# One order of slots from the first unit on, in a fused top-k attention and cosine feed-forward kernel

## The chip, the cores and the metric

The kernel runs on one core of one Trainium2 chip. Five engines work side by side, each through its own queue in order: TensorE (PE in the profile; PEld is its weight load), VectorE (DVE), ScalarE (ACT), GpSimd (POOL) and SyncE (SP), which here only issues DMA transfers. They wait for each other through semaphores. The metric is the time of one execution on the device in microseconds (us). Four executions of the kernel before took 1467.71, 1468.69, 1468.35 and 1466.98, median 1468.03. The profiled one is that of 1467.71, with a span of 1465.9 from its first to its last instruction.

## The reference, cut to what matters

```python
# q, k, v: (8 batches, 8 heads, 576 rows, 64), float32
scores = scale * np.matmul(q, k.transpose(0, 1, 3, 2))
kth = np.partition(scores, -top_k, axis=-1)[..., -top_k:-top_k + 1]      # top_k = 32
scores = np.where(scores >= kth, scores, -1000000000.0)
attn = np.exp(scores - np.max(scores, axis=-1, keepdims=True))
attn = attn / (np.sum(attn, axis=-1, keepdims=True) + 1e-09)
attn_out = np.matmul(attn, v).astype(np.float32)
# to (4608 tokens, 512), then
h = x @ w_in            # w_in (512, 2048)
g = h * np.cos(h)
out = g @ w_out         # w_out (2048, 512)
```

The two weight matrices reach the kernel as 64-bit floating point numbers, read as pairs of 32-bit words.

## The kernel before

**Units.** The tokens are cut into 36 tiles of 128, and the 8 heads into 4 pairs (NP = 4). A unit is one tile and one pair of heads, 144 in all (NU). A unit's scores are 128 x 2 x 576 numbers. Feed-forward work goes by blocks of 128 tokens, four units each: 8 first pieces (ff1, line 518: 16 matmul records to the profile's count) and 8 second pieces (ff2, line 599).

**Slots.** The order of the work is written out by hand: the loop at the end runs slots 0 to 144, and in slot i unit u = i is searched on VectorE, while unit w = i - 1 goes through its mask, exponentials and sums. Each engine runs its part of a slot in the order of the text. Three functions write slots: early_slot (line 696) for slots 0 to EARLY = 2 * NP = 8, slot (line 740) to LAST = 140, last_slot (line 787) for the rest.

**The search.** VectorE folds the 576 scores of a row into 288 maxima (fold_high, line 244) and 288 minima ("low"). It searches the maxima in four rounds of MAX8 and MATCH_REPLACE8 (lines 349 and 354, rounds 0 to 3 of topk_round), then the minima in two, and merges (lines 337 and 342). The minima are made in one of two ways: by VectorE from the scores in PSUM (fold_now, line 252), for units 0 to EARLY; or by GpSimd as sum minus maximum (fold_sum, line 262, and fold_low, line 271), for later units. ScalarE copies scores out of PSUM (take_scores, lines 233 and 234), masks (line 380) and exponentiates (line 388).

**Transposing the attention weights.** The product with v needs them transposed. For units before EARLY and the last four, transposes_now does it in the next slot: GpSimd normalises (line 409), TensorE transposes nine times (line 448), ScalarE copies to pT (lines 452, 455) and the product back out (line 485). For the others ("paired"), the way is through memory, two slots later: GpSimd splits the words in halves (split, lines 421 and 423), SP writes them to device memory (rows, line 431) and reads them back with a transposing DMA into pT (line 437, three buffers). Their values are then made by twos in every even slot (z: units i - 4 and i - 3), and VectorE multiplies them out by the reciprocal sums (take_values, line 483).

**Decoding the weights.** There are 32 chunks of 128 x 512 numbers: 16 of w_in, 16 of w_out. Each is loaded into one of 7 staging buffers (load_weights, line 102). Then decode_first: ScalarE turns the high words (line 128). decode_second: GpSimd rounds the low words (line 138) and VectorE shifts the high ones left by three (line 141). decode_third: GpSimd adds the two (line 151). early_slot handles three chunks a slot, two from slot 6 on; slot handles two.

**Feed-forward.** feed (line 643) issues pieces as a credit, their operands and the chunks decoded allow. After a first piece ScalarE takes the bank (lines 548 and 550), GpSimd reduces (570, 579), ScalarE takes the sine (589, with a table load to and fro) and GpSimd multiplies (gate, line 596); a second piece may follow.

In slot, the weights' steps stand here:

```python
        take_scores(units[i + 1])
        if w and not late:
            exponentials(w)
        decode_second(2)
        topk_round(u, 3, both(w), z)
        ...
        gate(1)
        ...
        decode_third()
        decode_first(2)
        reduce_first()
```

Of the kernel before, what the change touches and what calls it, by code (L numbers as in the profile page):

```python
# [30 lines left out]
def kernel(  # L31
# [62 lines left out]
    CHUNKS, XB = 7, 4  # L94
    ff = {"live": 0, "tick": 0, "now": 0, "credit": 0.0, "end": False, "kind": 0, "half": 0, "open": 0}
# [26 lines left out]
    def decode_first(n):  # L122


        for _ in range(min(n, len(wq["loaded"]))):
            st, w = wq["loaded"].popleft()
            hi = st[:, :, 1]
            nc.scalar.activation(
                out=w, in_=hi.bitcast(F32), func=AF.Prelu, scale=2.0**-111, alpha=2.0**32
            )  # L130
            wq["second"].append((st, w))

    def decode_second(n):

        for _ in range(min(n, len(wq["second"]))):
            st, w = wq["second"].popleft()
            wi, lo = w.bitcast(I32), st[:, :, 0]
            nc.gpsimd.tensor_scalar(
                out=lo, in0=lo.bitcast(U32), scalar1=2.0**-29, scalar2=1.0, op0=ALU.mult, op1=ALU.mult
            )  # L140
# [97 lines left out]
    def fold_high(u):  # L238

        s, sc = u["s"], u["sc"]  # L240
        if u["n"] > EARLY:
            del u["sc"]
# [23 lines left out]
    def fold_low(u):  # L266

        if not u["folds"]:
            return
# [19 lines left out]
    def topk_first(u, w):  # L289
# [5 lines left out]
        if u["folds"]:  # L295
            if u["n"] > EARLY:
                fold_sum(u)
# [5 lines left out]
        if u["folds"] and u["n"] <= EARLY:  # L303
            fold_now(u)
# [364 lines left out]
    EARLY, LAST = 2 * NP, NU - NP  # L669
    scored, last, last_values = {}, {}, {}  # L670
    for i, u in enumerate(units):
        two = i % 2 == 0 and EARLY + 2 < i < LAST + 2 and (len(u["parts"]) == 1 or u["hp"] == 0)
# [6 lines left out]
    for n in range(NP, len(order)):  # L679
        i = last[order[n - 5]] if n >= 5 else 0  # L680
        at_slot.setdefault(max(i, NP + 2), []).append((load_qk, *order[n]))
        i = last_values[order[n - 6]] if n >= 6 else 0
        at_slot.setdefault(max(i + 4 - i % 2, NP + 2), []).append((load_v, *order[n]))
# [7 lines left out]
    for i, u in enumerate(units):  # L691
        u["n"] = i
        u["folds"] = i < LAST + 2
        u["paired"] = EARLY <= i < LAST

    def early_slot(i, u, w):
        n = 3 if i < 6 else 2
        topk_first(u, w)
        if i == 0:
            decode_second(1)  # L700
        scores(units[i + 1])
        for load, b, hp in at_slot.get(i, []):
            load(b, hp)
        load_weights(n)
        if w:
            mask(w)
            exponentials(w)
        topk_round(u, 1)

        decode_second(n)  # L710
        topk_round(u, 2, both(w))
        topk_round(u, 3)
        if w:
            normalise(w)
        take_banks()
        take_scores(units[i + 1])
        gate(1)
        decode_third()
        feed(2)
        reduce_first()  # L720
        reduce_second()
        if i != NP:
            decode_first(n - 1)
        if w:
            transposes_now(w)
        feed(1)
# [170 lines left out]
```

## Time and profile before

| what | value |
|---|---|
| time, median of 4 | 1468.03 us (1466.98 to 1468.69) |
| the profiled execution's own time | 1467.71 us |
| its span | 1465.9 us |
| busy TensorE, VectorE, ScalarE, GpSimd | 1402.0, 1367.2, 1078.0, 1159.5 us |
| slots 0, 4, 8, 12, 16 start (first fold, line 244) at | 7.04, 52.72, 98.39, 142.96, 185.9 us |
| mean granted TensorE clock | 0.973 |

How to read it: a line of the timeline has the start, the length, the engine, the line of the kernel, the operation and its tiles, xN for N of them in a row, and in brackets how long the engine stood idle before it and what ended that. A line of a group has the total, the mean of one in ns, and the idle time before it with its releasers. A line by stretches has the busy time of each engine in that stretch. A busy TensorE is not TensorE at its peak, since matmuls overlap.

### The profile page before, as it was taken

Reading aid. Unit: us, or ns where it says so; the run is one execution under the profiler, and the core shown is the slowest. Engines: PE = TensorE matmul, PEld = TensorE weight load, DVE = VectorE, ACT = ScalarE, POOL = GpSimd, SP = SyncE. Lnnn points to the kernel's source line nnn. Section 1 sums busy time; section 2 is a strip of 40 time slices with the busy share of each in tenths; the row PEclk is TensorE's granted clock in tenths of the full one; section 3 lists DMA queues with packets and bytes.
Section 4 is the critical chain, followed back from the end, with each engine's and each line's share of the span. In section 5 each row is a group of like instructions: output and inputs, shape, how many; then the busy total and the mean of one; then the engine's idle time right before and its main releaser. Section 6 shows DMA issues by size and latency. Waiting matters only on the chain.

```text
span 1465.9 us, 30361 instructions
## 1 busy us (share of the span) xinstructions
PE 1402.0 (96%) x10360; PEld 1012.4 (69%) x10360; DVE 1367.2 (93%) x5209; ACT 1078.0 (74%) x1908; POOL 1159.5 (79%) x836
## 2 busy tenths in 40 slices
PE   4678899999999999999999999999999999999998
PEld 3565577777777767777777767777777777777765
DVE  7999999999999999999999999999999999999831
ACT  4666677777777777777777777777777787777651
POOL 4669888888888887888888888888888888888410
PEclk6688899999999999999999999999999999999999
DMA  8524576666664577557765667666666566655200
GB/s 278 153 90 141 149 200 162 156 162 187 174 174 143 150 196 181 159 145 189 190 166 142 159 171 197 168 147 168 194 176 152 149 161 176 168 152 147 66 8 15
DMA packets 405547, 229.53 MB, mean 157 GB/s; under 512 B 355088, under 2 KB 371728, under 8 KB 405392
## 3 DMA queue, kind: packets, MB, share of 16 engines
q1 hardware_dynamic: 399984, 217.93, 55.6%
q10 hardware_dynamic: 5408, 9.65, 1.8%
q8 instruction: 82, 1.34, 0.4%
q14 instruction: 73, 0.60, 0.1%
HBM read 45.09 MB, written 95.94 MB: 96 GB/s over the span
## 4 chain that ended last, share of the span: by engine, by line
PE 84%; DVE 6%; ACT 5%; DMA 2%; POOL 1%; issue 1%; SPq 1%; ACTq 0%; POOLq 0%
PE mm L534 32%; PE o L609 31%; PE rim L474 11%; PE sc L223 7%; DVE top L349 3%; PE rim L223 2%; DVE rest L354 2%; ACT s L388 1%; DMA v<-in_v_dram 1%; ACT s L380 1%; PE tp L448 1%; ACT L388 1%; ACT s L233 0%; DVE w_out L141 0%; DMA st<-in_moe_w_in_dram 0%
## 5 line engine op out<-in xcount | busy, mean ns | idle before, releaser
L534 PEld LDWEIGHTS mm<-xT,w_in 128*128 128x128 f32 x4608 | 540.4, 193 | 71.9 <-issue 65.8
L609 PE MATMUL o<-w_out,g 128*128 128x512 f32 x1152 | 541.1, 603 | 9.0 <-POOL g L596 6.0
L534 PE MATMUL mm<-xT,w_in 128*128 128x128 f32 x4608 | 543.0, 276 | 3.4 <-DVE xT L483 1.9
L349 DVE MAX8 top<-rest 128x8 f32<-128x288 f32 x1148 | 481.3, 454 | 0.0
L421 POOL COPY halves<-s 128x2304 uint16<-128x2304 uint16 x132 | 277.6, 2103 | 150.2 <-ACT s L388 150.0
L354 DVE MATCH_REPLACE8 rest<-top,rest 128x288 f32<-128x288 f32 (+1 forms) x860 | 376.9, 445 | 0.0
L609 PEld LDWEIGHTS o<-w_out,g 128*128 128x128 f32 x1152 | 203.4, 191 | 198.4 <-issue 186.6
L349 DVE MAX8 top<-low 128x8 f32<-128x288 f32 x568 | 239.3, 448 | 2.7 <-POOL low L271 2.7
L388 ACT ACTIVATE s<-s,nd 128x576 f32<-128x576 f32 x288 | 220.1, 766 | 0.8
L380 ACT ACTIVATE s<-s,top 128x576 f32<-128x576 f32 x288 | 206.1, 766 | 0.0
L271 POOL TENSOR_TENSOR low<-low,rest 128x576 int32<-128x576 int32 x133 | 187.8, 1412 | 10.4
L262 POOL TENSOR_TENSOR low<-s 128x576 int32<-128x576 int32 x133 | 187.6, 1411 | 1.3 <-DVE rden L401 1.3
L548 ACT ACTIVATE g<-mm 128x512 f32<-128x512 f32 x144 | 85.8, 596 | 130.5 <-PE mm L534 124.5
L474 PE MATMUL rim<-pT,v 128*64 128x128 f32 (+1 forms) x2560 | 161.9, 271 | 9.0 <-ACT pT L455 9.0
L579 POOL TENSOR_TENSOR x<-g,x 128x1024 f32<-128x1024 f32 x68 | 160.8, 2365 | 5.7
L596 POOL TENSOR_TENSOR g<-g,x 128x1024 f32<-128x1024 f32 x68 | 160.8, 2365 | 2.3 <-ACT x L589 2.3
L223 PE MATMUL sc<-k,q 64*128 64x448 f32 (+1 forms) x640 | 151.5, 584 | 9.2 <-DMA k<-in_k_dram 9.2
L474 PEld LDWEIGHTS rim<-pT,v 128*64 128x64 f32 x2560 | 134.3, 140 | 20.5 <-ACT pT L455 11.4
L233 ACT COPY s<-sc 128x896 f32<-128x896 f32 x144 | 129.2, 897 | 3.5 <-PE sc L223 3.0
L354 DVE MATCH_REPLACE8 low<-top,low 128x288 f32<-128x288 f32 x284 | 123.5, 443 | 0.0
L234 ACT COPY s<-rim 128x256 f32<-128x256 f32 x144 | 55.0, 382 | 84.9 <-PE rim L474 84.9
L244 DVE TENSOR_TENSOR rest<-sc,s 128x576 f32<-128x576 f32 x142 | 106.2, 748 | 6.1 <-ACT s L234 6.0
(59 smaller groups left out, 1323.0 us busy)
## 6 DMA issues: line engine op xcount, KB each, us to landing
rows<-halves SPq DMA_DIRECT2D x132, 640.0 KB, 3.0
out_dram<-ob ACTq DMA_DIRECT2D x36, 256.0 KB, 2.1
q<-in_q_dram SPq DMA_DIRECT2D x31, 288.0 KB, 3.9
st<-in_moe_w_in_dram SPq DMA_DIRECT2D x16, 512.0 KB, 6.0
v<-in_v_dram SPq DMA_DIRECT2D x32, 256.0 KB, 3.3
st<-in_moe_w_out_dram SPq DMA_DIRECT2D x16, 512.0 KB, 3.8
k<-in_k_dram SPq DMA_DIRECT2D x31, 144.0 KB, 3.6
k<-in_k_dram SPq DMA_DIRECT2D x32, 128.0 KB, 3.7
```

Source lines behind the costliest of these rows:

```text
L223: nc.tensor.matmul(to[r0 : r0 + rows, j, 0 : k1 - k0], st["q"][d, q0 : q0 + rows], st["k"][d, k0:k1], start=True, stop=True,)
L262: nc.gpsimd.tensor_tensor(out=u["low"].bitcast(I32), in0=s[:, :, 0:HS], in1=s[:, :, HS:S], op=ALU.add)
L271: nc.gpsimd.tensor_tensor(out=low, in0=low, in1=u["rest"][:, :, HS:S].bitcast(I32), op=ALU.subtract)
L349: nc.vector.max(to[:, j], src[:, j])
L354: nc.vector.match_replace(rest[:, j], to[:, j], src[:, j], NEG)
L380: nc.scalar.activation(out=s[:, j], in_=s[:, j], func=AF.Prelu, bias=less[:, j, 1:2], scale=1.0, alpha=FAR)
L388: nc.scalar.activation(out=s[:, j], in_=s[:, j], func=AF.Exp, bias=nd[:, j : j + 1], scale=SCALE, accum_out=den[:, j, 0:1],)
L421: nc.gpsimd.tensor_copy(out=halves[:, :, 0 : 2 * S], in_=s.rearrange("p (k h) -> p h k", h=2))
L474: nc.tensor.matmul(o[d, to], lhsT, rhs, start=c == 0, stop=c == NT)
L534: nc.tensor.matmul(mm[:, at : at + w], w_in[f // FC][:, c, (f % FC) * P : (f % FC + 1) * P], blk["xT"][:, c], start=c == 0, stop=c == NC - 1,)
L579: nc.gpsimd.tensor_tensor(out=x, in0=g, in1=x, op=ALU.subtract)
L609: nc.tensor.matmul(o, g[:, at : at + P], w_out[f], start=f == 0, stop=f == NF - 1)
```

## The change

- early_slot is gone; slot writes all slots up to 140. So units 0 to 7 too are transposed through memory, their values made by twos, two to three slots later, and multiplied out by VectorE; scores are made by twos from unit 4 on.
- The minima of units 7 to 10 (BUSY) are made by VectorE; those of all other units up to 141, the first seven included, by GpSimd.
- The low words of a chunk are rounded by ScalarE, in decode_first, in place of GpSimd in decode_second.
- All slots handle up to three chunks. Shifts and adds (decode_second, decode_third) now follow each other directly, behind round 2, that is behind the third of the four rounds; the adds stand ahead of the gate and reductions.
- In the first four slots the loads of q, k and v stand ahead of the chunks. Loads of the second batch are due from slot 10, not 6. Sines move to their later place from slot 12 on, not 16.

```diff
+    BUSY = range(7, 11)
...
-            hi = st[:, :, 1]
+            lo, hi = st[:, :, 0], st[:, :, 1]
             nc.scalar.activation(
                 out=w, in_=hi.bitcast(F32), func=AF.Prelu, scale=2.0**-111, alpha=2.0**32
             )
+            nc.scalar.mul(out=lo, in_=lo.bitcast(U32), mul=2.0**-29)
...
-            wi, lo = w.bitcast(I32), st[:, :, 0]
-            nc.gpsimd.tensor_scalar(
-                out=lo, in0=lo.bitcast(U32), scalar1=2.0**-29, scalar2=1.0, op0=ALU.mult, op1=ALU.mult
-            )
+            wi = w.bitcast(I32)
...
-        if u["n"] > EARLY:
+        if u["n"] not in BUSY:
             del u["sc"]
...
-        if not u["folds"]:
+        if not u["folds"] or u["n"] in BUSY:
             return
...
-            if u["n"] > EARLY:
+            if u["n"] not in BUSY:
                 fold_sum(u)
...
-        if u["folds"] and u["n"] <= EARLY:
+        if u["folds"] and u["n"] in BUSY:
             fold_now(u)
...
-        two = i % 2 == 0 and EARLY + 2 < i < LAST + 2 and (len(u["parts"]) == 1 or u["hp"] == 0)
+        two = i % 2 == 0 and 2 < i < LAST + 2 and (len(u["parts"]) == 1 or u["hp"] == 0)
...
-        at_slot.setdefault(max(i, NP + 2), []).append((load_qk, *order[n]))
+        at_slot.setdefault(max(i, 2 * NP + 2), []).append((load_qk, *order[n]))
...
-        u["paired"] = EARLY <= i < LAST
-
-    def early_slot(i, u, w):
...
+        u["paired"] = i < LAST
...
     def slot(i, u, w, x, z):
-        load_weights(2)
+        n = 3
+        if i < NP:
+            for load, b, hp in at_slot.pop(i, []):
+                load(b, hp)
+        load_weights(n)
         if x:
             send(x)
         topk_first(u, w)
         fold_low(u)
         topk_round(u, 1)
         topk_round(u, 2)
+        decode_second(n)
+        decode_third()
...
-        decoding = i < EARLY + 8
+        decoding = i < 3 * NP
...
-        decode_second(2)
         topk_round(u, 3, both(w), z)
...
-        decode_third()
-        decode_first(2)
+        decode_first(n)
...
-        if i <= EARLY:
-            early_slot(i, u, w)
-        elif i <= LAST:
+        if i <= LAST:
             slot(i, u, w, x, z)
```

## The prediction

> **What bounds the kernel now.** I read the page first: busy time and the forty slices.
>
> ```profile
> PE 1402.0 (96%) x10360; PEld 1012.4 (69%) x10360; DVE 1367.2 (93%) x5209; ACT 1078.0 (74%) x1908; POOL 1159.5 (79%) x836
> ...
> PE   4678899999999999999999999999999999999998
> ...
> DVE  7999999999999999999999999999999999999831
> ...
> PEclk6688899999999999999999999999999999999999
> ```
>
> TensorE is full from about the sixth slice on; before that VectorE is. The change touches only the first 13 or so of 144 units, so the question is how much earlier TensorE gets full. I call T(i) the start of slot i, read as VectorE's fold of unit i (line 244), and asked for the busy time of each engine slot by slot:
>
> ```profile
> 52.72:63.52 10.80, 6.11 (x37) 4.65 (x37) 10.77 (x41) 6.10 (x15) 7.17 (x9) 0.66 0.47 149
> 74.30:87.80 13.50, 13.50 (x127) 12.60 (x126) 10.43 (x40) 9.70 (x22) 6.59 (x8) 1.00 0.33 119
> 121.34:133.19 11.85, 11.85 (x72) 8.25 (x71) 11.85 (x38) 7.57 (x15) 11.53 (x10) 1.00 0.54 153
> 154.80:163.84 9.04, 5.94 (x21) 4.06 (x21) 9.04 (x36) 6.84 (x13) 7.68 (x6) 0.71 0.51 155
> 300.50:319.20 18.70, 18.70 (x139) 13.57 (x138) 18.48 (x74) 14.87 (x26) 16.10 (x12) 1.00 0.53 146
> ```
>
> The columns are the stretch, its length, busy PE, weight load, DVE, ACT, POOL, then granted clock, DMA share and GB/s. These are slots 4, 6, 10 and 13 and two settled slots (9.35 us each, TensorE full). A slot in which VectorE waits for nothing and shifts no weights takes it 9.05 us (slot 13). Where TensorE gets full for good is seen in the timelines of DVE and PE, in slot 14:
>
> ```profile
> 173.00 0.82 DVE L349 MAX8 top<-low 128x8 f32<-128x288 f32 x2 [2.71 <-POOL low L271]
> ...
> 174.59 0.48 DVE L483 TENSOR_TENSOR xT<-rim,pT 128x128 f32<-128x128 f32 x2
> ...
> 174.92 5.02 PE L534 MATMUL mm<-xT,w_in 128*128 128x128 f32 x28 [1.92 <-DVE xT L483]
> ```
>
> From 177 to 1345 us the table of waits has one of TensorE, 0.2 us long. Laid side by side, the written orders of the two kernels give out the same number of feed-forward pieces by the end of slots 8, 9 and 13 and the same in each slot from there (slot 14: one first, two second pieces). So the end moves by as much as this first piece of slot 14 (174.92) moves, and by nothing later: I follow VectorE to it.
>
> **The lock that decides.** VectorE's shift of a weight chunk (line 141) takes 0.42 us, 1.00 for three in line, unless GpSimd is at work:
>
> ```profile
> 57.43 1.09 DVE L141 TENSOR_SCALAR w_in<-w_in 128x512 int32<-128x512 int32 x3
> ...
> 126.99 2.93 DVE L141 TENSOR_SCALAR w_out<-w_out 128x512 int32<-128x512 int32 x2
> 129.85 0.81 DVE L349 MAX8 top<-rest 128x8 f32<-128x288 f32 x2
> ```
>
> ```profile
> 125.70 1.41 POOL L138 TENSOR_SCALAR st<-st 128x512 int32<-128x512 uint32 x2
> 127.19 2.45 POOL L596 TENSOR_TENSOR g<-g,x 128x1024 f32<-128x1024 f32 x1
> ```
>
> ```profile
> L141 DVE TENSOR_SCALAR w_out<-w_out x16: 408/424/2601, 68.6 to 149.5; 128x512 int32<-128x512 int32 x16
> ```
>
> At 127 us one shift ran, the waiting GpSimd gate went next, and the second shift took 2.60 us: it waited the gate out. Three of the four late pairs (115.18, 126.99, 148.60) took 2.7, 2.9 and 2.5 us, 5.9 more than three free pairs of 0.75; so the shifts already pay for GpSimd.
>
> **The change, part by part.**
>
> *Folds and outputs.* Nine fold_now (0.67 apart, line 252) become four: VectorE -3.3 us. Eight units' outputs are now multiplied by VectorE, two in 0.40 us (line 483): +1.6.
>
> *GpSimd.* Roundings gone: 32 x 0.659 = -21.1. Normalising of eight units gone: 16 x 0.785 = -12.6. Splits for them: 8 x (2.10 + 0.40) = +20.0. Folds of five more units: 5 x 2.82 = +14.1. Sum +0.4, but in another order. Its slot is now split 2.5, folds 2.8, three adds 3.9 (1.30 each), in all 9.2, and in slots 7 and 8 reductions of 3.4 instead of the folds. From T(i) the folds end at about +4.6 to +5.3 and the shifts, now behind the third round, come at +5.65 (slot 16: 185.90 to 191.54). So the first shift finds GpSimd idle. That is the gain of the move: the 5.9 us.
>
> *The adds directly behind the shifts.* Before, other GpSimd work stood between. Now add 1 waits for shift 1 alone. After shift 1 GpSimd started its add 0.14 us (117.56 to 117.70) and about 0.2 (139.3 to 139.51) later, so at +0.56 to +0.62; shift 2 starts at +0.34 and lets go at about +0.65; shift 3 would start at +0.67. By the 127 us row the waiting GpSimd operation goes first, and shift 3 waits 1.27 us for an add. Bounds: 0 (shift 3 first), 2.55 (two adds first). The order is a matter of 0.1 us; I take 1.27, for the row shows that very contest.
>
> The Trainium skill, "SBUF — State Buffer", "Who interferes with whom", calls the port pair of the two engines an exclusive lock, held for a whole instruction by whoever issues first. The 2.60 us agree. Read so that three queued shifts count as issued together, it would give 0 instead of 1.27 and a time of 1456 instead of 1466; read by the start times above, it gives 1.27 as well.
>
> *Roundings on ScalarE.* No row shows them. Nearest are the decode on the same engine and shape (0.682 and 0.695 alone, 0.58 apart in line) and its 512-wide copies (0.58); I take 0.6 (0.57 to 0.70), 3 a slot = 1.8. Gone are the copies of line 452, 455 and 485, about 1.6 a slot. ScalarE has 6.1 to 7.8 busy in slots of 10.8, and its softmax sums are now wanted only behind the last low search. I cost it at nothing, the cover being that slack; in slots 8 and 9, with sines and table loads, it has 11 to 12 us in slots of 10.4 to 12.4. Uncovered: 0 to 2 us. Waiting behind the roundings are the mask and exponentials of the next slot.
>
> *TensorE.* Of 108 transposes (341 ns in the row of 96) 72 go. In slots 1 to 4, 7 and 8 TensorE idles; only in slots 5 and 6 were they in its way (1.3 us each). I cost them at nothing; upper gain 2.6.
>
> *Transfers.* Eight times rows out and transposed back, in SP's queue between the chunk loads:
>
> ```profile
> rows<-halves SPq DMA_DIRECT2D x132, 640.0 KB, 3.0
> ...
> st<-in_moe_w_in_dram SPq DMA_DIRECT2D x16, 512.0 KB, 6.0
> ...
> pT<-rows SPq DMA_TRANSPOSE x132, 4.9
> ```
>
> A unit's share is 4.1 to 4.6 us of all DMA engines (slots 12 to 14: 0.38 x 11.84, 0.51 x 9.04, 0.34 x 12.19), three chunks 4.7 to 5.1 (slots 3, 4): 9.5 in slots of 11.3 and more, about 84%. A unit is written and transposed by about +10 to +13 of its slot and wanted in the next even slot at +7.7. Cost nothing, cover 3 to 5 us. Loads of the second batch move from slots 6 to 10; it is first scored in slot 14. Nothing.
>
> *First pieces later.* Block 0 is complete in slot 6, not 4; slot 7 gets five pieces with no scores behind them. This takes away the wait of slot 6 (3.04 us for the exponentials at 83.17, behind TensorE's pieces). In slot 9 the first gate stands behind two adds (about 121.0 to 123.4), then four second pieces (7.6 at a waking clock, as 5.40 and about 2 at 117), scores 2.6 and values 2.5: outputs at 136.1, wanted by VectorE at 132.6. Wait 3.6 in slot 10 (0 to 5).
>
> **The sum.** Slot 0 has its wait for chunk landings (T(1) = 18.1, was 18.91). Slots 1 to 3 and 5: 9.05 + 1.00 + 1.27 = 11.3. Slots 4, 6: + 0.40 = 11.7. Slot 7: 11.3 + 0.67 = 12.0; slot 8: 12.4. Slot 9, two shifts: 9.05 + 0.70 + 0.67 = 10.4. Slot 10: 12.4 + 3.6. Slots 11 to 13: 9.05, 9.45, 9.05. That gives T(2) 29.5, T(5) 63.8 (was 63.52), T(9) 111.3 (was 109.53), T(11) 137.7 (was 133.19), T(14) 165.2 (was 163.84). Slot 14 has no late fold (weights' work has left GpSimd after slot 10), so its outputs come at +8.1: 173.3 against 174.92. Gain 1.6 us. The profiled execution took 1467.71, 0.3 under the median of 1468.03: 1467.71 - 1.6 + 0.3 = 1466.4. TensorE's own work from the gate's end at 123.4 to that piece is 18 pieces of 1.75, six units' scores (1.3) and values (1.25), 47 us: it would be there at about 171, so with the gate at 123.4 the gain is 4 us at most.
>
> **The rivals.** About 0.2%, 2.9 us, is what a measurement can tell from no change.
>
> *B, shift 3 is never held.* Slots 1 to 8 and 10 lose the 1.27: 11.4 us less, of which slot 10's wait takes back 1.1: 1456. For it: the margin is 0.1 us. Against it: the 2.60 us row. DMA at 9.5 of 10.1 us a slot would take some back; 1456 to 1460.
>
> *C, two adds go before shift 3* (the second is ready when the first ends, as shift 3 is). Another 1.27 in nine slots, 11.4: 1478; it ends slower from about 0.5 us a slot on. For it: nothing waits between adds. Against it: at 148.60 a shift got in between two GpSimd operations.
>
> *D, the transfer chain sets the slots.* Rows landing behind three chunks in 6.0 instead of 3.0, then transposed 4.9 and the next loads issued 1.6 gives 12.5 a slot instead of 11.5 in slots 3 to 8: +6: 1472. It decides once the outputs of a pair wait for their transposed rows past +7.7 of an even slot. Against it: slack of 3 to 5 us to eat first.
>
> **How the numbers follow.** My case (one add) 0.50: from 1460 to 1471, with the unknowns of slot 10 (-3.6 to +1.4), ScalarE (+2) and transposes (-2.6); a third of it is under 1465.1. B 0.24, C 0.13, D 0.13. Faster: 0.18 + 0.23 + 0.01 = 0.42. Within 0.2%: 0.27 + 0.01 + 0.04 = 0.32. Slower: 0.26. Leaving out the far end of B and C, the range is 1456 to 1475.
>
> **What would show it.** In the changed profile: line 140's shifts with a median near 0.42 and every third one near 1.7 (mine), all 0.42 (B) or near 3 (C); T(5) near 64 and T(9) near 111; a wait of VectorE for outputs in slot 10; TensorE without gaps from about 173. The forecast is wrong if T(9) is under 106, or if waits for DMA appear before line 473.

## The result, and the profile after

The changed kernel took 1471.66 us (median of 34 runs, 1467.48 to 1475.76), the kernel before 1467.93 (median of 55). The ratio is 1.0023 with an interval of 1.0018 to 1.0028: slower, by 3.4 to 3.7 us, where 1466.4 and faster was forecast. The profiled execution took 1470.72 with a span of 1468.9, 3.0 more than before.

The page of the changed kernel, busy times and slices:

```profile
PE 1386.7 (94%) x10288; PEld 1000.9 (68%) x10288; DVE 1365.1 (93%) x5212; ACT 1088.5 (74%) x1910; POOL 1164.7 (79%) x814
...
PE   3376899999999999999999999999999999999998
...
DVE  8898999999999999999999999999999999999831
...
PEclk6578999999999999999999999999999999999999
DMA  8787566656665566656755656656666556755300
```

VectorE and GpSimd have as much to do as before and TensorE less, and yet TensorE is full no sooner. The row that has changed most is that of the transfers: it begins with 8787566, where before it had 8524576.

Below are slots 4, 6, 10 and 13 and two settled slots, by stretches (the length, busy PE, weight load, DVE, ACT, POOL, granted clock, DMA share, GB/s), to be laid beside the rows shown of before:

```profile
48.58:61.47 12.89, 7.03 (x48) 5.21 (x48) 10.49 (x42) 8.01 (x16) 9.59 (x8) 0.50 0.84 247
73.59:87.02 13.43, 8.12 (x57) 6.36 (x58) 13.43 (x42) 8.12 (x16) 10.46 (x8) 0.63 0.80 248
122.65:138.56 15.91, 15.41 (x85) 8.84 (x86) 11.11 (x42) 10.65 (x17) 11.31 (x9) 0.86 0.75 215
156.94:166.68 9.74, 9.07 (x68) 7.27 (x66) 9.10 (x36) 9.62 (x16) 5.46 (x4) 1.00 0.56 163
303.26:321.95 18.69, 18.69 (x139) 13.56 (x138) 18.47 (x74) 14.88 (x26) 16.11 (x12) 1.00 0.53 142
```

The settled slots are unchanged (18.69 for 18.70). In slots 4 and 6 the DMA share rose from 0.47 and 0.33 to 0.84 and 0.80, and the rate from 149 and 119 GB/s to 247 and 248. In slot 4 VectorE is idle for 2.4 us of 12.89. The slots by their starts (VectorE's fold, line 243 now), with what the prediction gave each:

| stretch | before | predicted | after | after less predicted |
|---|---|---|---|---|
| T(1) | 18.91 | 18.1 | 17.80 | -0.3 |
| slots 1 to 3 | 33.81 | 33.9 | 30.78 | -3.1 |
| slots 4 to 6 | 35.08 | 34.7 | 38.44 | +3.7 |
| slots 7 and 8 | 21.73 | 24.4 | 22.11 | -2.3 |
| slot 9 | 11.81 | 10.4 | 13.52 | +3.1 |
| slot 10 | 11.85 | 16.0 | 15.91 | -0.1 |
| slots 11 to 13 | 30.65 | 27.6 | 28.12 | +0.6 |
| slot 14 up to its first piece | 11.08 | 8.1 | 11.11 | +3.0 |
| first piece of slot 14 at | 174.92 | 173.3 | 177.79 | +4.5 |

Where VectorE stood, in its timeline (start, length, and in brackets the idle time before and what ended it):

```profile
58.44 0.82 DVE L348 MAX8 top<-low 128x8 f32<-128x288 f32 x2 [2.40 <-POOL low L270]
...
70.96 0.82 DVE L348 MAX8 top<-low 128x8 f32<-128x288 f32 x2 [2.03 <-POOL low L270]
...
79.25 4.11 DVE L140 TENSOR_SCALAR w_out<-w_out 128x512 int32<-128x512 int32 x3
...
115.41 2.84 DVE L140 TENSOR_SCALAR w_out<-w_out 128x512 int32<-128x512 int32 x2
...
137.11 0.49 DVE L482 TENSOR_TENSOR xT<-rim,pT 128x128 f32<-128x128 f32 x2 [4.80 <-ACT s L233]
...
175.86 0.82 DVE L348 MAX8 top<-low 128x8 f32<-128x288 f32 x2 [2.72 <-POOL low L270]
```

In slots 4 and 5 it waits for GpSimd's minima, in slot 6 GpSimd's work holds its shifts (4.11 us for three), in slot 9 again (2.84 for two), in slot 10 it waits for outputs and in slot 14 for minima. GpSimd's timeline shows why it is late in the first of these:

```profile
52.16 2.10 POOL L420 COPY halves<-s 128x2304 uint16<-128x2304 uint16 x1 [3.22 <-DMA rows<-halves]
...
64.73 2.10 POOL L420 COPY halves<-s 128x2304 uint16<-128x2304 uint16 x1 [2.58 <-DMA rows<-halves]
...
76.31 2.10 POOL L420 COPY halves<-s 128x2304 uint16<-128x2304 uint16 x1 [1.63 <-DMA rows<-halves]
...
88.70 2.10 POOL L420 COPY halves<-s 128x2304 uint16<-128x2304 uint16 x1 [2.95 <-DMA rows<-halves]
```

The split of a unit waits until the rows of the unit before it have left the one `halves` buffer. From 25 to 115 us rows took 7.8 us from issue to landing (rows and chunks of the list of DMA issues in that stretch); over the whole run it is 3.0, as in the kernel before:

```profile
st<-in_moe_w_in_dram SPq DMA_DIRECT2D x9, 512.0 KB, 6.2
rows<-halves SPq DMA_DIRECT2D x7, 640.0 KB, 7.8
pT<-rows SPq DMA_TRANSPOSE x7, 4.8
```

On SyncE a slot then is: issue the chunks 1.5, wait for the rows to land 7.8, issue the transposes 2.7, in all 12.0. The transposes were issued at 52.06, 64.63, 76.66, 88.72, 101.07 and 113.44, every 12.0 to 12.6 us, while VectorE alone needs 10.0 (slots 2 and 3). The minima and the adds come behind the split on GpSimd, and VectorE behind those. TensorE, too, waits for transposed rows ahead of slot 9, once each in slots 4, 6 and 8 (the table of its waits from 5 to 110 us):

```profile
PE rim L473 <- DMA pT<-rows: 7.7, 3, 2.9
```

At the other end, TensorE's timeline shows its two long waits:

```profile
122.99 9.18 PE L608 MATMUL o<-w_out,g 128*128 128x512 f32 x16 [12.40 <-POOL g L595]
...
177.79 5.02 PE L533 MATMUL mm<-xT,w_in 128*128 128x128 f32 x28 [4.31 <-DVE xT L482]
```

The second is the piece from which TensorE is full: 177.79 against 174.92, 2.9 us later; the span is 3.0 longer.

### The profile page after: what moved, and what is told of

It is laid out like the page before. It is cut to its first block, busy times and chain, and to the rows that moved or that the text cites. A ratio compares the mean times of both kernels' runs of the same rounds, so it can differ in the third digit from the quotient of the medians.

```text
span 1468.9 us, 30250 instructions
## 1 busy us (share of the span) xinstructions
PE 1386.7 (94%) x10288; PEld 1000.9 (68%) x10288; DVE 1365.1 (93%) x5212; ACT 1088.5 (74%) x1910; POOL 1164.7 (79%) x814
## 4 chain that ended last, share of the span: by engine, by line
PE 84%; DVE 8%; ACT 3%; DMA 2%; POOL 2%; issue 1%; SPq 0%; ACTq 0%; POOLq 0%
PE o L608 32%; PE mm L533 32%; PE rim L473 10%; PE sc L222 8%; DVE top L348 3%; PE rim L222 2%; DVE rest L353 2%; ACT s L387 1%; DMA st<-in_moe_w_in_dram 1%; DMA v<-in_v_dram 1%; DVE w_out L140 1%; DMA rows<-halves 1%; DVE rest L243 1%; ACT s L379 0%; ACT L387 0%
## 5 line engine op out<-in xcount | busy, mean ns | idle before, releaser
L608 PE MATMUL o<-w_out,g 128*128 128x512 f32 x1152 | 538.5, 601 | 13.6 <-POOL g L595 12.4
L420 POOL COPY halves<-s 128x2304 uint16<-128x2304 uint16 x140 | 294.5, 2103 | 166.7 <-ACT s L387 153.7
L270 POOL TENSOR_TENSOR low<-low,rest 128x576 int32<-128x576 int32 x138 | 195.0, 1413 | 10.8
L261 POOL TENSOR_TENSOR low<-s 128x576 int32<-128x576 int32 x138 | 195.5, 1417 | 6.2 <-ACT s L233 4.1
L222 PEld LDWEIGHTS sc<-k,q 64*128 64x128 f32 (+1 forms) x640 | 46.5, 181 | 101.6 <-DVE rest L353 47.8
```

The costliest lines, as they stand in the source:

```text
L222: nc.tensor.matmul(to[r0 : r0 + rows, j, 0 : k1 - k0], st["q"][d, q0 : q0 + rows], st["k"][d, k0:k1], start=True, stop=True,)
L261: nc.gpsimd.tensor_tensor(out=u["low"].bitcast(I32), in0=s[:, :, 0:HS], in1=s[:, :, HS:S], op=ALU.add)
L270: nc.gpsimd.tensor_tensor(out=low, in0=low, in1=u["rest"][:, :, HS:S].bitcast(I32), op=ALU.subtract)
L420: nc.gpsimd.tensor_copy(out=halves[:, :, 0 : 2 * S], in_=s.rearrange("p (k h) -> p h k", h=2))
L608: nc.tensor.matmul(o, g[:, at : at + P], w_out[f], start=f == 0, stop=f == NF - 1)
```

## The experiments

All ratios are to the kernel before, measured beside it. T(18) is the start of slot 18, when TensorE has long been full: 204.27 before, 207.13 after.

### What the transfers cost

*A quarter of each chunk is loaded, and decoded four times over; three quarters of the weights are left out.*

```diff
-            nc.sync.dma_start(out=st.rearrange("p w i -> p (w i)"), in_=src)
+            nc.sync.dma_start(out=st[:, 0 : CW // 4].rearrange("p w i -> p (w i)"), in_=src[:, 0 : CW // 2])
...
-            lo, hi = st[:, :, 0], st[:, :, 1]
+            lo = st[:, :, 0]
+            hi = st[:, 0 : CW // 4, 1].unsqueeze(1).to_broadcast([P, 4, CW // 4])
...
-            nc.scalar.mul(out=lo, in_=lo.bitcast(U32), mul=2.0**-29)
+            nc.scalar.mul(out=lo.rearrange("p (a c) -> p a c", a=4), in_=hi.bitcast(U32), mul=2.0**-29)
```

> The changed kernel, with a quarter of each chunk loaded (128 KB instead of 512) and decoded four times over, so that all engines have the same work; three quarters of the weights are left out. Theories L and V both: slots 2 to 8 take 10.0 to 10.7 us, T(9) is 100 to 102 (109.1 with whole chunks), rows land in 3 to 4 us. On the end: if the transfers are what made the change slower, 1461 to 1464; by G (first gate in slot 9 and late fold in slot 14 set the end) 1468 to 1471.

Measured: 1459.66 us, 0.9945 (0.9932 to 0.9958). Rows land in 3.0, slots 4 to 8 take 10.0 to 11.0, T(9) is 98.89 for 109.13. With fewer bytes and otherwise the same instructions the new order is 8 us faster than the kernel before; the bytes take 11 to 12 us from it. (The same was not tried on the kernel before, which waits for chunks in slot 0 as well, so some of the 8 may not belong to the change.) Slots 4 to 6 take 30.77 us for 38.44, slot 9 10.29 for 13.52. Three waits stay: 14.1 us of TensorE before the first gate, 5.5 of VectorE for the outputs in slot 10, 2.7 in slot 14.

*The chunks are loaded through ScalarE's queue.*

```diff
-            nc.sync.dma_start(out=st.rearrange("p w i -> p (w i)"), in_=src)
+            nc.scalar.dma_start(out=st.rearrange("p w i -> p (w i)"), in_=src)
```

> The changed kernel, with the chunk loads issued from ScalarE's queue instead of SyncE's; the same transfers and volume. In the changed kernel the transposes of a unit followed those of the unit before by 12.0 to 12.6 us five times running, whichever engine then waited. Theory L (a loop through the one queue: transposes issued 2.7, then three loads 1.5, then rows landing behind them 7.8): without the loads in it the loop is under 10, slots 4 to 8 take 10.5 to 11, T(9) is 100 to 104, rows land in 3 to 5 us; time 1463 to 1466. Rival V (volume: 10 us of all DMA engines a slot, 0.80 to 0.84 of it): slots 4 to 8 still take 12 or more, T(9) 108 or more; time 1470 to 1474, and ScalarE pays about 1.5 us a slot for the issues.

Measured: 1479.07, 1.0080 (1.0063 to 1.0097). The stretch from 38 to 88 us in the changed kernel:

```profile
38.00:88.00 50.00, 21.45 (x125) 14.61 (x126) 45.57 (x163) 32.94 (x65) 39.44 (x29) 0.53 0.81 237
```

with the chunks on the second queue:

```profile
38.00:88.00 50.00, 16.59 (x92) 10.36 (x92) 45.66 (x162) 33.20 (x66) 37.28 (x29) 0.55 0.98 247
```

and with a quarter of the chunks:

```profile
38.00:88.00 50.00, 29.05 (x207) 23.42 (x204) 50.00 (x192) 38.36 (x77) 42.59 (x33) 0.65 0.65 175
```

The last three columns are the clock, the DMA share and the rate. A second queue fills the DMA engines (0.98) and moves 4% more. Rows land in 5.8, but the transposes take 8.8 to 10.5 instead of 4.8. So it is not the order of SyncE's queue alone that costs 12 us a slot. A slot of 12.5 us at 237 GB/s is 3.0 MB, and with another queue the same bytes take no less time (slots 4 to 8 12.9 us in the mean, 12.1 in the changed kernel). The time of 1479.07 is not the price of a second queue alone: ScalarE now issues the loads, T(1) is 5.0 us later than in the changed kernel, and ScalarE waits for chunks (2.47 us at 55.43).

*The other three ways to move the wait.* The rows ahead of the chunks in SyncE's queue:

```diff
-        load_weights(n)
         if x:
             send(x)
+        load_weights(n)
```

> The changed kernel, with the three chunk loads of a slot issued behind the rows' write and transpose instead of ahead of them; the same transfers, the same volume. Theory Q (the rows of a unit queue behind three chunk loads, land in 7.8 us, hold the one halves buffer, and so make GpSimd's split, its folds and VectorE late): rows land in 3 to 4 us in slots 2 to 9, GpSimd's wait for rows falls from 10.6 us to under 2, VectorE's waits of 2.4 and 2.0 for the late folds in slots 4 and 5 are gone, T(9) is 100 to 102 instead of 109.1. Rival V (the transfers' volume, about 80% of all DMA engines): rows land in 6 us or more, T(9) is 107 or more, the time stays at 1471. On the end Q alone says that what VectorE gains is kept: 1463 to 1465. Rival G (the end is set by the feed-forward's first gate in slot 9 and the late fold in slot 14, whatever T(9) is): T(9) early, but the time not under 1468.

Measured: 1477.2, 1.0060 (1.0045 to 1.0075). Rows land in 5.6 (30 to 120 us) and GpSimd's split no longer waits for them, but chunks come late: slots 4 to 8 take 13.49, 12.85, 12.39, 12.50 and 11.97.

Four more units' minima on VectorE, so that GpSimd has slack:

```diff
-    BUSY = range(7, 11)
+    BUSY = range(4, 11)
```

> The changed kernel, with the minima of units 4 to 6 made by VectorE too (range(4, 11)), so that no late fold of GpSimd can hold VectorE in slots 4 to 6; transfers as they were. Theory Q: VectorE pays 3 x 0.67 = 2.0 us and saves the waits of 2.4 and 2.0 and the held shifts of slot 6 (3.1): T(9) 103 to 106. Rows still land in about 7.8 us, and outputs may now wait for transposed rows. Rival V: outputs wait for their transposed rows as long as the folds did, T(9) 108 or more. Time 1466 to 1469 by Q if the end follows T(9), 1470 to 1472 by G.

Measured: 1473.19, 1.0026 (1.0010 to 1.0042), as the changed kernel. Slots 4, 6 and 8 take 13.76, 13.35 and 14.20: VectorE now waits for outputs (5.9 us in three waits), whose values wait for transposed rows (5.2 us in one wait of TensorE behind 100 us).

Two buffers for the split words (the room is taken from xT):

```diff
-        halves = work.tile([P, 2, 2 * S + P], U16, tag="halves", name="halves", bufs=1)
+        halves = work.tile([P, 2, 2 * S + P], U16, tag="halves", name="halves", bufs=2)
...
-            blk["xT"] = work.tile([P, NP, P], F32, tag="xT", name="xT", bufs=5)
+            blk["xT"] = work.tile([P, NP, P], F32, tag="xT", name="xT", bufs=3)
```

> The changed kernel with two halves buffers instead of one (and three instead of five buffers for the blocks' inputs, to make room). The split of a unit no longer waits for the rows of the unit before to land. Theory Q: GpSimd's wait for rows goes from 10.6 us to near 0 though the rows still land in 7 us or more; folds are in time, T(9) 101 to 104 unless transposed rows come late for the outputs. If the buffer is not what holds GpSimd, T(9) stays near 109. Time 1463 to 1467 by Q, 1470 to 1472 by G.

Measured: 1474.24, 1.0042 (1.0029 to 1.0054). The split never waits, and the outputs do, as the table of VectorE's waits from 30 to 120 us says:

```profile
DVE xT L482 <- ACT s L233: 9.0, 3, 4.5
```

None of the three comes near the time that its first theory gave. Each edit mends the wait that it is aimed at, and another stands in its place of about the same size: the mean of slots 4 to 8 is 12.3 to 12.6 us in the three and 12.1 in the changed kernel.

Two chunks a slot from slot 4:

```diff
-        load_weights(n)
+        load_weights(n if i < 4 else 2)
```

> The changed kernel, with two chunks loaded a slot from slot 4 on instead of three; all else follows (32 chunks are done in slot 13 instead of 10, one feed-forward piece comes two slots later). Theory V (the transfers' volume sets slots 4 to 9: 3.0 MB a slot moved at some 240 GB/s take 12.3 us, whatever the order or queue; a quarter of a chunk instead of a whole one made them 10.0): 2.5 MB take 10.4, slots 5 to 9 are 10.2 to 11.2, T(9) is 102 to 105 (109.1 with three), rows land in 4 to 6 us; the time 1465 to 1468. Rival: it is the latency of the loop of rows, transposes and loads and not volume: slots stay at 11.5 or more, time 1470 or more.

Measured: 1477.45, 1.0056 (1.0041 to 1.0071). The rate falls to 207 GB/s and T(9) to 105.95; slots 5 to 9 take 11.2 us in the mean, between the theory (10.2 to 11.2 each) and its rival (11.5 or more). T(11) is 133.82 for 138.56. Then it is all lost in slot 12, which takes 20.11. The time is over both the 1465 to 1468 of the theory and the changed kernel's. The timelines of TensorE, ScalarE and SyncE:

```profile
138.23 3.84 PE L533 MATMUL mm<-xT,w_in 128*128 128x128 f32 x32 [0.41 <-ACT x L549]
...
150.62 3.78 PE L533 MATMUL mm<-xT,w_in 128*128 128x128 f32 x16 [8.55 <-ACT x L549]
```

```profile
146.42 0.67 ACT L129 ACTIVATE w_out<-st 128x512 f32<-128x512 f32 x1 [5.65 <-DMA st<-in_moe_w_out_dram]
```

```profile
142.19 1.00 SPq L116 DMA_DIRECT2D st<-in_moe_w_out_dram  x2
```

TensorE waits for ScalarE to take a bank, and ScalarE, whose work goes in the order of the text, stands before that at the decoding of a chunk. With two chunks a slot, chunks are still being loaded here, and their load stands in SyncE's queue behind the queries, keys and values of the second batch, which are issued from 135.28 to 142.1. So the loss is again one of transfers, and the run does not show what two chunks a slot would be worth with those loads elsewhere.

### ScalarE's rounding

*Alone on the kernel before:*

```diff
-            hi = st[:, :, 1]
+            lo, hi = st[:, :, 0], st[:, :, 1]
...
+            nc.scalar.mul(out=lo, in_=lo.bitcast(U32), mul=2.0**-29)
             wq["second"].append((st, w))
...
-            nc.gpsimd.tensor_scalar(
-                out=lo, in0=lo.bitcast(U32), scalar1=2.0**-29, scalar2=1.0, op0=ALU.mult, op1=ALU.mult
-            )
```

> The kernel before, with one part of the change alone: low words rounded by ScalarE at the end of decode_first. Theory: GpSimd loses 21 us of work in slots 0 to 12, the gates of slots 9 to 12 come 1.3 us sooner and hold fewer shifts, ScalarE has room: 1465 to 1468. Rival: ScalarE's 1.8 us more in each early slot delay the copies of the transposes and the mask behind them: slots 2 to 6 grow by up to 0.5 each, 1469 to 1471.

Measured: 1468.45, 1.0005 (0.9995 to 1.0014), no change, though GpSimd loses 21 us of work.

*Taken back in the changed kernel* (GpSimd rounds in decode_second, the rest as changed):

> The changed kernel, with the low words rounded by GpSimd in decode_second again. Theory: GpSimd has 2.0 us more to do in each slot up to 10, but in slots 4 to 9 it waited 2 to 3 us for rows; what is not covered is the first three slots, where roundings stand ahead of the adds and the split: 0 to 4 us slower than the changed kernel, 1471 to 1475. Rival: the roundings, running as VectorE comes to its shifts, hold one shift a slot by 0.65 to 1.3 and make the folds late: 6 to 10 us slower, 1477 to 1481.

Measured: 1475.44, 1.0045 (1.0032 to 1.0058), some 0.2% above the changed kernel; the profiled first fold of slot 14 is 0.7 us later. So the rounding on ScalarE is worth something only in the new order, in which GpSimd carries the split and the folds of the first units.

### Slot 14

*Unit 14's minima on VectorE, in the kernel before:*

```diff
-        if u["n"] > EARLY:
+        if u["n"] > EARLY and u["n"] != 14:
             del u["sc"]
```

(the same condition in fold_sum, fold_low and fold_now).

> The kernel before, with the minima of unit 14 made by VectorE. Both kernels wait 2.7 us in slot 14 for GpSimd's fold, after which TensorE is full. Theory: VectorE pays 0.67 and the wait goes: slot 14 takes 10.0 instead of 12.19, the first piece of slot 14 starts at about 172.8 instead of 174.92, time 1465.5 to 1466.5. Rival: TensorE, not VectorE, has the work of this stretch to do and the wait for keys in slot 18 grows: 1467.5 to 1468.5.

Measured: 1466.73, 0.9996 (0.9987 to 1.0004). The wait of 2.71 us is gone: slot 14 takes 10.07 for 12.19, and T(18) is 201.79 for 204.27. Yet of these 2.5 us about 0.6 are seen at the end, 1.9 at most by the interval.

*The same in the changed kernel, with the rows first:* BUSY = (7, 8, 9, 10, 14) and the order of the first of the three edits above.

> As the first run, and the minima of unit 14 made by VectorE too, which pays 0.67 us and cannot wait 2.7 for GpSimd's fold in slot 14. Theory: the wait of slot 14 is a separate one, so this adds a gain of about 2 us to that of the first run: T(14) to its first piece 8.8 us instead of 11.1; 1461 to 1463. Rival: what holds GpSimd in slot 14 (its reductions, behind ScalarE) or ScalarE itself then holds the next thing, and the time stays with the first run.

Measured: 1475.32, 1.0045 (1.0032 to 1.0057). Slot 14 takes 10.02. The time is 1.9 us under that of the rows first alone (1477.2), but the intervals overlap, so the gain is not shown.

### The adds behind the gate again

```diff
         decode_second(n)
-        decode_third()
         made = scored.get(i, [])
...
+        decode_third()
         decode_first(n)
```

> The changed kernel, with the adds behind the gate again (only slots 9 and 10 have both, so that only there the order of GpSimd changes). Theory: the gate of slot 9 ends 2.6 us sooner, so the second pieces, the scores behind them and slot 10's outputs come sooner: slot 10 13.3 to 14 instead of 15.91, time 1469 to 1470. Rival: the gate waits for ScalarE's sine or for the split, and holds the shifts: no gain, 1471 to 1473.

Measured: 1472.23, 1.0023 (1.0013 to 1.0032), as the changed kernel. But the head is better: TensorE waits 10.0 instead of 12.4 for the first gate, slot 10 takes 13.24 for 15.91, and T(18) is 204.10, 3.0 less than the changed kernel and 0.2 less than the kernel before.

*With two chunks from slot 4 and unit 14's minima on VectorE as well* (the three edits above together):

> As the run with two chunks from slot 4 on, with the adds behind the gate again (as in the kernel before) and the minima of unit 14 made by VectorE. Theory: the three waits are apart and in a chain, so each counts: TensorE's wait for the first gate in slot 9 (12.4 us, 14.1 with quarter chunks) shrinks by 2.6, VectorE's wait in slot 14 by 2; time 1461 to 1464, under both kernels. Rival: the gate now stands in the way of the shifts (2.4 held in slots 9 to 12, as in the kernel before) and takes its 2.6 back: 1464 to 1467.

Measured: 1474.68, 1.0038 (1.0026 to 1.0051). Slot 14 takes 10.02, but slot 12 still 18.81: ScalarE waits 6.17 us there for a chunk, and TensorE 8.55 for ScalarE.

### Why a gain ahead of slot 18 does not reach the end

The runs on slot 14 and on the adds say that something behind slot 18 gives gains back. I laid the starts of all slots side by side for the fourteen profiles taken up to here. From slot 18 on all but four slots take the same in each, to within 0.1 us (slots 106 and 107 apart, which are up to 0.3 longer in four of them). Slots 18, 54, 90 and 126 do not:

| kernel | slot 18 | 54 | 90 | 126 | sum | T(18) |
|---|---|---|---|---|---|---|
| before | 11.63 | 10.64 | 11.03 | 10.26 | 43.56 | 204.27 |
| changed | 11.52 | 10.45 | 11.66 | 10.41 | 44.04 | 207.13 |
| before, unit 14 on VectorE | 11.77 | 10.58 | 11.41 | 10.51 | 44.27 | 201.79 |
| changed, adds late | 12.29 | 11.88 | 11.94 | 10.45 | 46.56 | 204.10 |

In the timeline of weight loads, at the scores of slot 18 in the kernel before:

```profile
207.60 0.20 PEld L223 LDWEIGHTS sc<-k,q 64*64 64x64 f32 x4 [0.76 <-DVE top L349]
208.18 0.19 PEld L223 LDWEIGHTS sc<-k,q 64*64 64x64 f32 x2 [0.38 <-issue]
209.30 0.13 PEld L223 LDWEIGHTS sc<-k,q 64*64 64x64 f32 x1 [0.94 <-DMA k<-in_k_dram]
```

and in the changed kernel with the adds late:

```profile
207.86 0.20 PEld L222 LDWEIGHTS sc<-k,q 64*64 64x64 f32 x4 [0.76 <-DVE rest L353]
209.28 0.19 PEld L222 LDWEIGHTS sc<-k,q 64*64 64x64 f32 x2 [1.23 <-DMA q<-in_q_dram]
209.79 0.13 PEld L222 LDWEIGHTS sc<-k,q 64*64 64x64 f32 x1 [0.32 <-DMA k<-in_k_dram]
```

The unit scored in these slots (19, 55, 91, 127) is the last of the four whose tile is cut between two batches. The queries and keys of its new batch were asked for only at the end of the slot before, when the scores of the unit before it had freed their buffers, and in SyncE's queue they stand behind that slot's transposes. In slot 54 the last load of keys was issued 0.27 us into the slot in the kernel before, and 1.40 with the adds late; the slot is 1.24 longer. This is a place that neither the prediction nor its rivals had. The test: a sixth buffer for the keys, asked for one pair earlier, the room taken from xT (three buffers of xT left the four slots at 44.78 in the run with two buffers for the split words, so room taken there gains nothing by itself).

```diff
-        k = st["k"] = loads.tile([P, S], F32, tag="k", name="k")
+        k = st["k"] = loads.tile([P, S], F32, tag="k", name="k", bufs=6)
...
-            blk["xT"] = work.tile([P, NP, P], F32, tag="xT", name="xT", bufs=5)
+            blk["xT"] = work.tile([P, NP, P], F32, tag="xT", name="xT", bufs=4)
...
-        at_slot.setdefault(max(i, NP + 2), []).append((load_qk, *order[n]))
+        at_slot.setdefault(max(i, NP + 2), []).append((load_q, *order[n]))
+        i = last[order[n - 6]] if n >= 6 else 0
+        at_slot.setdefault(max(i, NP + 2), []).append((load_k, *order[n]))
```

On the kernel before:

> The kernel before, with a sixth buffer for the keys of a pair and their load asked for one pair earlier; the queries' load stays where it is (the room comes from xT, four buffers for five). In every profile so far the four slots 18, 54, 90 and 126 take 10.3 to 12.3 us where their neighbours take 9.3 to 9.5, and before TensorE's weight load of the scores stands a wait for the keys (0.82 and 0.94 us in two of the four slots of before). Theory K, the keys are late there: the four slots take about 10.3 each, 41.3 together for 43.56, and the time falls by about 2.3 us: ratio 0.9985 (0.998 to 0.9995). Theory M, the four slots are long because their unit is scored in two parts, with more matmuls: they keep 43 to 44 together, and the ratio is 1.000. If the queries are what comes last, the wait is named for them and half is gained.

With unit 14's minima on VectorE too:

> The same keys, with unit 14's minima on VectorE as in the earlier run on the kernel before (slot 18 began 2.5 us earlier there, the four slots took 44.27 together, the ratio was 0.9996). Theory K: both gains are kept, slot 18 begins at about 201.8, the four slots take 41.3, and the profiled time is about 1465.99 - 3.0 = 1463: ratio 0.9965 (0.9955 to 0.998). Theory M: as that run, 0.9996.

On the changed kernel with the adds late:

> The changed kernel with the third step's adds back behind the gate, and the keys one pair earlier. Without the keys slot 18 began at 204.10, 0.2 us before the kernel before, and yet the ratio was 1.0023, with 46.56 in the four slots against 43.56. Theory K: the four slots take 41.3, the profiled time is about 1472.38 - 5.3 = 1467, ratio 0.999 (0.998 to 1.0), within 0.1% of the run with the keys on the kernel before. Theory M: 1.0023 stays.

And that with unit 14's minima on VectorE:

> The run before this one, with unit 14's minima on VectorE too (slot 14 then takes 10.0 for 12.2). Theory K: slot 18 begins at about 201.9, the four slots take 41.3, ratio 0.9975 (0.996 to 0.999), about the same as the kernel before with both edits. Theory M: 2.2 us under the 1.0023, about 1.001.

| keys earlier, on | time | ratio | four slots | T(18) |
|---|---|---|---|---|
| before | 1462.49 | 0.9959 (0.9947 to 0.9971) | 40.04 | 201.84 |
| before, unit 14 | 1460.96 | 0.9952 (0.9939 to 0.9965) | 40.34 | 200.93 |
| changed, adds late | 1466.9 | 0.9987 (0.9978 to 0.9996) | 41.22 | 206.70 |
| changed, adds late, unit 14 | 1465.64 | 0.9982 (0.9972 to 0.9993) | 42.30 | 203.74 |

The weight loads of the first of these, at the scores of slot 18:

```profile
204.32 0.20 PEld L232 LDWEIGHTS sc<-k,q 64*64 64x64 f32 x4 [0.76 <-DVE rest L363]
205.05 0.20 PEld L232 LDWEIGHTS sc<-k,q 64*64 64x64 f32 x3 [0.53 <-DMA q<-in_q_dram]
```

Theory K holds for the four slots: in this run no wait ends with the keys any more, half a microsecond for the queries is left, and the slots fall by 3.5 on the kernel before (43.56 to 40.04) and by 5.3 with the adds late (46.56 to 41.22). Theory M is out. Two of the forecasts missed: on the kernel before the ratio came out under its range (0.998 to 0.9995), and the two orders, which were to be equal, are 0.3% apart. On the kernel before the head won 2.4 us besides (T(18) 201.84); of these 1.2 are in slot 6, where VectorE's wait for the exponentials fell from 3.04 to 1.82, and that the earlier loads do this was not looked into. With the adds late, T(18) is 2.6 later in the profile with the keys than in that without, as much as its slot 8 is longer (14.26 for 11.64); that is one profile each, and was not followed further.

Two things follow. The second of the four runs is the fastest kernel here that computes all, 6.8 us under the kernel before and beyond both kernels compared. And once both have their keys earlier the new order is behind the old one by 4.4 us (1466.9 against 1462.49) and 4.7 (1465.64 against 1460.96), even with its adds late. In the new order slot 18 still waits for the queries, 1.06 and 1.87 us at the weight loads, and the four slots together are 1.2 and 2.0 us longer than in the old one (41.22 for 40.04, 42.30 for 40.34). That is part of the difference; the larger part lies ahead of slot 18 (T(18) 206.70 for 201.84, 203.74 for 200.93), so the late keys are not what made the change slower.

## Why the prediction was wrong

It said faster by 1.6 us; the kernel became 3.4 us slower. By its own steps, with the table of slots above:

**"Transfers. Cost nothing, cover 3 to 5 us."** This is the step that failed most. The 84% were a sum of shares that each kind of transfer shows when it runs apart from the other, and the rest was read as room enough; the cover is the time from a unit's transposes to their use, and says nothing of the buffer that its rows hold until they land. The sum itself was near: 0.81 of the DMA engines over a mean slot of 12.1 us is 9.8, where 9.5 was given. But chunks, rows and transposes wait for each other in one queue: rows landed in 7.8 us instead of 3.0, and a round took 12.0 to 12.6; with a second queue the engines are full at 0.98 for 4% more. In slots 4 to 6 this is +3.7 us against the prediction. The transfers' own cost there is larger, for the prediction had also paid there for a third shift that is mostly not held: a quarter of the bytes makes these slots 7.7 us shorter and the kernel 12 us faster (1459.66 against 1471.66). Rival D came near (12.5 a slot, 1472) and was given 0.13, but in part it was luck: its 12.5 is 6.0 for the rows, 4.9 until the transposes land and 1.6 for the next loads, where the round was 7.8, 2.7 and 1.5, and its 1472 starts from slots of 11.5 us that take 10.0 to 11.0 with a quarter of the bytes. Its place was wrong as well: it should have decided "once the outputs of a pair wait for their transposed rows". The prediction's own sign, "waits for DMA appear before line 473", did appear, 7.7 us of TensorE in three waits, but up to slot 9 VectorE lost only 0.37 us to late outputs; its long waits for outputs in these slots came when another buffer or other minima had been given. In the changed kernel the wait came in at the one `halves` buffer, a resource that neither the sum nor the rival had looked at, because in the kernel before its rows land in 3.0 us.

**"I take 1.27" for the third shift.** Wrong; it is rival B's zero. Where GpSimd is on time (slots 1 to 3, 7, 8 and 10) the third shift is not held. VectorE's and GpSimd's timelines in slot 3:

```profile
44.23 1.09 DVE L140 TENSOR_SCALAR w_in<-w_in 128x512 int32<-128x512 int32 x3
```

```profile
44.78 4.16 POOL L150 TENSOR_TENSOR w_in<-w_in,st 128x512 int32<-128x512 int32 x3 [0.57 <-DVE w_in L140]
```

Three shifts take 1.09 us, and it is the adds that wait, 4.16 for three instead of 3.8. Slots 2 and 3 take 10.0 us and slots 1 to 3 3.1 less than predicted. The Trainium skill, "SBUF — State Buffer", "Who interferes with whom", says that whoever issues first holds the shared port pair for the whole instruction. Read so that three queued shifts count as issued together, this was the reading of the prediction that gave 0, and these rows agree with it. They do not settle the rule. In slot 6 (79.25), where the late split pushed GpSimd's folds onto the shifts, the second shift waited for a fold and the third for an add (1.61 and 1.51 us), as the prediction had it. In slot 9 (115.41) a split that had started 0.08 us earlier, late behind reductions that waited for ScalarE, held the first shift (2.30). And in slot 5, where a fold starts 0.03 us behind the first of three shifts, it is again the fold that waits (2.32 us for 1.41):

```profile
67.14 2.32 POOL L261 TENSOR_TENSOR low<-s 128x576 int32<-128x576 int32 x1
```

By their recorded starts the cases look alike: the gate of the 2.60 us row starts 0.13 us ahead of the shift that it holds, the add in slot 3 0.12 ahead of the third shift, which goes first. What decides between them is not shown.

**"That is the gain of the move: the 5.9 us."** Mostly lost. The move was to let the shifts find GpSimd idle. With GpSimd late they were held for 3.1 us in slot 6 and 2.1 in slot 9, 5.2 in all.

**"Slot 14 has no late fold."** Wrong. VectorE waits 2.72 us at 175.86, as long as before (2.71). The reason given, that the weights' work has left GpSimd, is true and does not matter; in the kernel before it had left by then too (the last add is at 152.48). GpSimd's reductions wait 4.61 us there for ScalarE, which switches its table and is busy with exponentials:

```profile
167.09 1.04 POOL L569 TENSOR_SCALAR x<-x 128x1024 f32<-128x1024 int32 x1 [4.61 <-ACT x L549]
168.22 2.39 POOL L578 TENSOR_TENSOR x<-g,x 128x1024 f32<-128x1024 f32 x1
170.55 2.11 POOL L420 COPY halves<-s 128x2304 uint16<-128x2304 uint16 x1
```

and split and folds stand behind them. ScalarE's rounding in the kernel before left the wait at 2.73; VectorE's minima for unit 14 take it away. It is 3.0 us of the 4.5 by which the first piece of slot 14 was missed.

**Slot 9, "two shifts: 10.4".** It took 13.52: the 2.84 of the held shifts, and a GpSimd that waits 3.24 for ScalarE at 111.89 and is late with everything behind. With a quarter of the bytes the slot takes 10.29, so this loss, too, goes with the transfers; by which way was not followed.

**Slot 10, "wait 3.6 (0 to 5)".** Right in place and kind: TensorE waits 12.4 for the gate behind the adds, and VectorE 4.80 for the outputs. The slot was given 16.0 and took 15.91.

**T(9), T(11) and T(14)** were given as 111.3, 137.7 and 165.2 and came at 109.13, 138.56 and 166.68. That is near, and it means little: an overestimate of 5.4 us in slots 1 to 3, 7 and 8 and an underestimate of 6.8 in slots 4 to 6 and 9 lie under it. A test that is passed at the sums can fail in every term.

**"The end moves by as much as this first piece of slot 14 moves, and by nothing later."** For this change it held in the profiled executions: +2.9 at the piece, +3.0 at the span, with +0.5 from the four slots of late keys. As a rule it fell: with the adds late the head won 3.0 and the four slots took 2.5 of it and the end nothing. The one TensorE wait of 0.2 us that the prediction found behind 177 us was the trace of it. The rest of these waits sits at the weight loads, and in matmuls that seem longer (2.25 us for seven that took 1.10 elsewhere), which the table of TensorE's own waits does not show.

**ScalarE's rounding "at nothing"** held as a term: the roundings take 0.66 us each and start 0.57 behind the decode ahead of them (0.6 was given), VectorE's waits for ScalarE in slots 1 to 3 are 0.33 and 0.26 us, and alone the rounding changes nothing.

## What to carry to other kernels

Do not add up the DMA shares that transfers have in different stages and call the rest free, even where the sum is right: find the resource that a transfer holds until it lands (here one buffer and a queue), put the longer landing time into its round trip, and compare the round trip with the slot. When each mended wait is followed by another of the same size, look for the shared supply behind them, and take away a part of its volume rather than one more wait. And when an engine looks full, compare the lengths of equal steps along the run: four slots that were 1 to 3 us longer than their neighbours held about as much as the whole change.

## What the runs showed of the hardware

- Transposes alone fill the DMA engines at 290 GB/s (share 0.9 and more, a settled slot of the kernel before at 600 us), rows alone at 410 to 430. Mixed with chunk loads, on two queues, the engines were 0.98 busy at 247 GB/s, and a transpose took 8.8 to 10.5 us instead of 4.8. The Trainium skill, "DMA: Bandwidth & Descriptors", "Latency and other measured facts", has 261 GB/s for a transposing DMA with a non-contiguous middle dimension and about 350 to 400 for the contiguous case; the 290 of transposes alone lie between, and which case this kernel's are was not worked out.
- Three shifts of VectorE in line all went ahead of a GpSimd add that became ready after the first (1.09 us for three, the adds 0.37 longer), and of a fold that started 0.03 us behind the first (2.32 us for 1.41). Elsewhere a GpSimd operation got in between two shifts (2.60 us for one shift in the kernel before, 1.61 and 1.51 in slot 6 of the changed one), or held the first of them when it had started ahead (2.30). What decides is not shown.
- A late transfer behind a full TensorE shows as a longer matmul group and as a wait of the weight load, hardly as a wait of the matmul: 0.94 and 1.23 us at the weight loads of slot 18 (the kernel before, and the changed one with the adds late), against 0.2 and 0.7 us for keys in the whole table of TensorE's waits behind slot 10.
